# A fused attention and two feed-forward layers on one core: one-bank PSUM tiles for the tanh layer's products, and side work at its two ends moved

## The chip, the core and the metric

The kernel runs on one core of one Trainium2 chip. The metric is device microseconds of one execution, the median of several runs. A core has TensorE (PE in the profile, with its weight loads shown apart as PEld), VectorE (DVE), ScalarE (ACT), GpSimd (POOL) and SyncE (SP, which here issues nearly all DMAs). TensorE writes its products into PSUM, which has eight banks of 512 float32 values per partition; everything else lies in SBUF.

## What is computed

Three layers follow each other, over 4 sequences of 3072 tokens with 256 channels, all in float32:

```python
scores = (1/S) * z @ z.T                  # z: (4, 3072, 64)
x1 = u * (np.maximum(scores, 0)**2 @ v)   # attention, one 3072 x 3072 block per sequence
h  = x1 @ w_in                            # (12288, 256) @ (256, 2048)
x2 = (h - np.tanh(h)) @ w_out             # (12288, 2048) @ (2048, 256): the tanh layer
xk = mu_k*x2 + (1-mu_k)*x2_prev           # x2_prev: the token before, zero at a sequence's start
xr = mu_r*x2 + (1-mu_r)*x2_prev
out = sigmoid(xr @ w_r) * (np.maximum(xk @ w_k, 0)**2 @ w_v)
```

## The kernel before

Every matrix product is taken in three passes of 128x128 by 128x512 over operands split into a high and a low part (`PASSES`), so a product of one 128x128 block is three matmuls. Tokens are worked in 24 tiles of 512. A hand-written order (`tc.manual_schedule()`) sets what stands on each engine's queue; a tile framework adds the waits. An engine works its queue strictly in order, so an instruction that waits holds up all behind it. There are three stages.

Stage A, attention, 288 units (`A`). A unit makes the scores of 256 keys against 512 queries, and its products with `v` are issued two units later (`LAG`). Half of the score blocks are not computed again but loaded back from DRAM transposed; their names are `t` (`h_t`, `l_t`) instead of `A`. Computed blocks that are needed again are transposed by VectorE (`k`) and stored.

Stage S, the tanh layer, 96 units (`h_unit`, called H in the profile's names). A unit n = 8 i + j takes token tiles 2i and 2i+1 and the hidden blocks j and j+8, and computes the four 128x512 blocks of h by seven block products instead of eight. Two PSUM accumulators `e` and `a`, one bank each, hold partial sums, and each of the seven products of three matmuls stands at a fixed place in the unit: `a` gets A11, `e` gets A12; then `a` gets S2 and `e` gets S1; then `e` gets S4 and `a` gets S3; last `a` gets -A22. Between these groups values are taken out: ScalarE copies the first `a` into `r1`, VectorE adds `e` to it; ScalarE copies both into `rc`, and VectorE adds the later `e` and `a` to it crosswise. Tanh is taken of r1 and rc and of the last `a`; VectorE subtracts (`less`), ScalarE takes the high part and VectorE the low part (`h_split`), twice in a unit: `Hx` (h_Hx, l_Hx, of `gx`) and `Hy` (of `gy`). `e` and `a` are the halves of one two-bank tile `w_H`, of which there are two.

The products with `w_out` are issued one unit later, as a list `q` of 24 single matmuls (`h_piece`, six for each of the four blocks of h) that fills TensorE while the other engines empty the accumulators. `cuts` says how many of them stand behind A12, behind S1, and behind S3. In most units the first twelve are Hx pieces; in the unit with j = 0 the list is six Hx pieces, then twelve Hy pieces; with j = 1 the same order. The Hy parts of unit n are made early in unit n+1.

Stage K, the channel mix, per token tile four units `K` and one `R`, again with LAG 2 and squares split into parts.

Side work (loading and splitting weights, preparing x1 as `x`, `xh`, `xd`, `xo`; mixing x2 as `mx`, `mk`, `mr`) is put in by `task(first, last, steps, ...)`: `run_steps(n)` issues steps while a budget per unit lasts, or as many as stand over once `last` has come. `load(n, ...)` issues DMAs at the start of unit n. In the tanh layer `run_steps` is called behind the second group of pieces, so its VectorE steps stand ahead of the `rc` additions. `L718` is the addition into r1, `L738` that into rc, `L631` the copies, `L635` tanh, `L638` the subtraction, `L87` and `L90` the high and low parts, `L625` the block products, `L658` the w_out pieces, `L610` the products of stages A and K, `L562` those of R.

Of the kernel before, what the change touches and what calls it, by code (L numbers as in the profile page):

```python
# [7 lines left out]
F32 = mybir.dt.float32  # L8
# [4 lines left out]
ALU = mybir.AluOpType  # L13

P = 128
# [4 lines left out]
def relu2_attention__tanh_ffn__channel_mix_kernel(  # L20
# [23 lines left out]
    nc = tc.nc  # L44
# [18 lines left out]
    ps = ctx.enter_context(tc.tile_pool(name="ps", bufs=2, space=bass.MemoryType.PSUM))  # L63
# [347 lines left out]
    PASSES = ((0, 0), (0, 1), (1, 0))  # L411
    acc, split = {}, {}

    def work(name):
        return ps.tile([P, 2, 512], F32, tag="wk", name=name, bufs=2)

    def parts(name):
        h = sb.tile([P, 2, 512], F32R, tag="hi", name=f"h_{name}", bufs=3)
# [3 lines left out]
    def scratch(name):  # L422
        return sb.tile([P, 2, 512], F32, tag="e", name=name, bufs=5)
# [164 lines left out]
    def pieces_of(unit):  # L588
        kind, t, p = unit
        if kind == "R":  # L590
            return []
        s = split.pop(unit)
        o = get_acc(kind, t)
        last = {"A": NP, "K": NK}[kind] - 1
        w = []
        for j in range(2):
            f = 2 * p + j
            if kind == "A":
                kp = pairs[t % NG][p]
                f = kp // 2 * 4 + kp % 2 + 2 * j  # L600
                w.append([vs[t // NG, f // 4][:, l, f % 4] for l in range(2)])
            else:
                w.append([x[:, f % 4] for x in ws["v", f // 4]])
        order = [(j, c) for j in range(2) for c in range(DC)]
        if unit == ("K", NT - 1, NK - 1):
            order.sort(key=lambda x: x[1])

        def one(j, c, n):
            a, m = PASSES[n]
            nc.tensor.matmul(  # L610
                o[c],
                w[j][a][:, c * P : (c + 1) * P],
                s[m][:, j],
                start=p == 0 and j == 0 and n == 0,
                stop=p == last and j == 1 and n == 2,
            )

        return [lambda x=(j, c, n): one(*x) for j, c in order for n in range(3)]
# [11 lines left out]
    def copied(t, a):  # L630
        nc.scalar.activation(out=t, in_=a, func=ACTF.Copy)  # L631
        return t
# [4 lines left out]
    def less(g, h):  # L637
        nc.vector.tensor_tensor(out=g, in0=h, in1=g, op=ALU.subtract)  # L638

    def swapped(x):  # L640
        step, n = x.ap[1]
        return bass.AP(x.tensor, x.offset + step, [x.ap[0], (-step, n), *x.ap[2:]])

    hp, hb = {}, {}

    def h_piece(n, half, t):
# [58 lines left out]
    def h_unit(n, q):  # L705

        i, j = divmod(n, NHF)
        if "g" not in hb:
            g = sb.tile([P, 2, 2, 512], F32, tag="big", name="g_H", bufs=12)
            hb["g"] = [g[:, 0], g[:, 1]]  # L710
        gx, gy = hb["g"]
        cuts = [len(q) * 6 // 24, len(q) * 14 // 24]
        w = work(f"w_H{n}")
        e, a = w[:, 0], w[:, 1]
        product(a, i, j, "A11", "B11", True, False)
        product(e, i, j, "A12", "B21", True, True)
        r1 = copied(p2(f"r1_{n}"), a)
        nc.vector.tensor_tensor(out=r1, in0=e, in1=r1, op=ALU.add)  # L718
        if n:
            low = h_split("y")  # L720
            less(gx[:, 0], hb.pop("a"))
            low()
        tanh(gx[:, 1], r1)
        less(gx[:, 1], r1)
        for f in q[: cuts[0]]:
            f()
        product(a, i, j, "S2", "T2", False, False)
        product(e, i, j, "S1", "T1", True, False)
        rc = copied(scratch(f"rc_{n}"), w)
        for f in q[cuts[0] : cuts[1]]:  # L730
            f()
        run_steps(NA + n)
        hb["x"] = (n, 0 if n else 1, 2, ((n - 1, 1, 0) if n else None, (n, 0, 0)), gx)
        low = h_split("x")
        empty()
        product(e, i, j, "S4", "B22", False, True)
        product(a, i, j, "S3", "T3", False, False)
        nc.vector.tensor_tensor(out=swapped(rc), in0=w, in1=swapped(rc), op=ALU.add)  # L738
        low()
        for f in q[cuts[1] :]:  # L740
            f()
        empty()
        tanh(gy, rc)
        less(gy, rc)
        hb["y"] = (n, 0, 2, ((n, 1, 1), (n, 0, 1)), gy)
        product(a, i, j, "-A22", "T4", False, True)
        tanh(gx[:, 0], a)
        hb["a"] = a

    def h_end(n):  # L750
        gx = hb["g"][0]
        low = h_split("y")
        less(gx[:, 0], hb.pop("a"))
        low()
        hb["x"] = (n, 0, 1, ((n - 1, 1, 0), None), gx)
        h_split("x")()
# [83 lines left out]
    NHF = NH  # L840
    NS = NT // 2 * NHF
    units = [("A", t, p) for t in range(NT) for p in range(NP)]
    NA = len(units)
# [3 lines left out]
    NB = NA + NS  # L847
    at = {x: n for n, x in enumerate(units)}
# [19 lines left out]
    for t in range(NT):  # L868
        n = t * NP + (-7 if t % NG == NG - 1 else 1 if t else 5)
# [6 lines left out]
    for b in range(1, B):  # L876
        prev = (b - 1) * NG * NP
        last = prev + (NG - 1) * NP
        for g in range(NG):
            n = last + LAG + (-18, -6, 3, 6, 9, 11)[g]  # L880
            load(n, v_load, b, g)
            task(n + 3, min(n + 12, b * NG * NP + 2 * g + LAG - 2), v_steps, b, g)
        for g in range(NG):
            n = prev + 2 * NP + 7 * g
# [11 lines left out]
    for n, x in enumerate(halves):  # L896
        k = c0 + n * (c1 - c0) // len(halves)
# [4 lines left out]
    def weights(n, end, *x):  # L902
        load(n - (1 if NA < n < NB else 2), w_load, *x, n)
        task(n, end, w_steps, *x)
# [6 lines left out]
    for s in range(2):  # L911
        n = last - 42 + 6 * s
# [6 lines left out]
    for k, n in enumerate((NA + 1, NA + 2, NA + 3, NA + 2)):  # L919
        pieces(n, n, 1, k)  # L920
    weights(NA + 4, NA + 4, "out", 1)
    weights(NA + 4, NA + 4, "out", 3)
    n = NB - NHF
    weights(n + 2, n + 3, "r", 0)
    weights(n + 4, n + 5, "k", 0)
    weights(n + 4, n + 5, "k", 1)
    weights(n + 5, n + 6, "v", 0)
    weights(n + 5, n + 6, "v", 1)
    for i in range(NT // 2):
        n = NA + NHF * i  # L930
        load(n - 6 if i else n - 9, x_load, i)
        task(n - 5 if i else n - 8, n - 1, x_steps, i)
    for i in range(NT):
        n = at["K", i, 0]
        load(n - 5 if i else n - 3, x2_load, i)
        task(n - 4 if i else n - 2, n - 1, mix_steps, "k", i)
        task(n - 3 if i else n - 2, at["R", i, 0] - 1, mix_steps, "r", i)
        n = at["K", i, NK - 1] + LAG
        task(n, n + 2, out_steps, i)
    tasks.sort(key=lambda x: x[:3])  # L940
# [24 lines left out]
    with tc.manual_schedule():  # L965
        z_load(0, 0)
        z_load(0, 1)
        v_load(0, 0)
        z_load(0, 2)
        v_load(0, 1)  # L970

        zeros = scratch("zeros").bitcast(F32R)[:, 0]
        nc.gpsimd.memset(zeros.bitcast(F32), 0.0)
        idle = work("idle")
        for j in range(11):
            nc.tensor.matmul(idle[:, j % 2], zeros[:, :P], zeros, start=True, stop=True)
        for cost, f in z_steps(0, 0) + z_steps(0, 1):
            f()
        for m, src in ((0, moe2_mu_k), (1, moe2_mu_r)):
            with nc.allow_non_contiguous_dma(reason="a column of the mixing vector"):  # L980
                nc.sync.dma_start(out=mu[:, m, :], in_=src.rearrange("(c p) -> p c", p=P))
        def begin(n):
            for f in loads.pop(n, ()):
                f()
            if n in stores:
                stores.pop(n)()

        for n in range(NA):
# [36 lines left out]


# [27 lines left out]
```

## Time and profile before

| | |
|---|---|
| three runs | 2577.86 us median (2577.7 to 2578.09) |
| the profiled execution | 2580.78 us, span 2578.8 us |
| stage A, 0 to 944.9 us | PE busy 938.17, DVE 769.87, ACT 668.81 us; DMA share 0.81 |
| tanh layer, 944.9 to 1971.5 us | PE busy 1013.94, DVE 725.14, ACT 618.60 us; DMA share 0.09 |
| stage K, 1971.5 us to the end | PE busy 597.56, DVE 398.60, ACT 303.32 us; DMA share 0.19 |
| mean granted TensorE clock | 0.997 |
| chain that ended last | PE 90%, DVE 4%, ACT 3%, DMA 1%, issue 1% |

A matmul's busy time is not what it costs. One of 128x512 is shown with about 0.39 us, but the next one starts 0.23 us after it, so they overlap. What TensorE loses shows as a longer step from one start to the next, and only partly as idle time.

### The profile page before, as it was taken

The numbers are of one execution on the slowest core, as the hardware profiler recorded it, in microseconds if no ns is written. First come the engines' busy times: TensorE is split into PE (matmuls) and PEld (weight loads), VectorE is DVE, ScalarE is ACT, GpSimd is POOL, SyncE is SP. The second block draws the span as 40 slices with busy tenths as digits, with TensorE's granted clock in tenths as the row PEclk, the third lists the DMA queues.
The fourth block names the chain that finished last, engine by engine and source line by source line (L and its number), as shares of the span: only waits on it lengthen the run. The fifth ranks groups of instructions, "written<-read, shape, count | busy, mean of one in ns | idle before, by whom it ended". The sixth has DMA issues, their size and how long they took to land.

```text
span 2578.8 us, 29584 instructions
## 1 busy us (share of the span) xinstructions
PE 2549.7 (99%) x11051; PEld 2069.3 (80%) x11051; DVE 1893.6 (73%) x2363; ACT 1590.7 (62%) x1973; POOL 17.5 (1%) x53
## 2 busy tenths in 40 slices
PE   9999999999999999999999999999999999999999
PEld 7888888888888877777777777777777888888887
DVE  8887888888888767677766776677667576676665
ACT  7766776776687666566556655565566455454553
POOL 0000000000000000000000000000000000000000
PEclk9999999999999999999999999999999999999999
DMA  7798689669958860000000000000010112111111
GB/s 192 228 221 216 192 227 226 197 191 238 245 171 277 217 169 28 33 33 15 19 33 34 28 6 33 33 33 1 33 62 25 41 42 49 42 41 45 46 41 33
DMA packets 382784, 260.17 MB, mean 101 GB/s; under 512 B 263984, under 2 KB 337712, under 8 KB 382640
## 3 DMA queue, kind: packets, MB, share of 16 engines
q1 hardware_dynamic: 379472, 257.89, 36.9%
q8 instruction: 86, 1.41, 0.2%
q10 hardware_dynamic: 3168, 0.39, 0.1%
q14 instruction: 58, 0.48, 0.1%
HBM read 142.87 MB, written 109.31 MB: 98 GB/s over the span
## 4 chain that ended last, share of the span: by engine, by line
PE 90%; DVE 4%; ACT 3%; DMA 1%; issue 1%; SPq 0%; ACTq 0%; DVEq 0%
PE acc_A L610 29%; PE w_H L625 19%; PE acc_H L658 15%; PE w_K L547 10%; PE acc_K L610 10%; PE w_A L524 3%; PE w_A L523 3%; PE w_R L562 3%; DVE r L718 3%; ACT r L631 2%; DMA b<-at 1%; DMA zin<-in_z_dram 0%; SPq L105 0%; DVE rc L738 0%; DVE xo_T L90 0%
## 5 line engine op out<-in xcount | busy, mean ns | idle before, releaser
L610 PE MATMUL acc_A<-h_A,v 128*128 128x512 f32 x1344 | 441.1, 390 | 0.3 <-ACT h_A L87 0.3
L625 PE MATMUL w_H<-xo_T,w_in 128*128 128x512 f32 x1152 | 322.1, 401 | 12.7 <-DVE rc L738 5.3
L610 PE MATMUL acc_A<-h_t,v 128*128 128x512 f32 x960 | 309.8, 389 | 0.0
L610 PEld LDWEIGHTS acc_A<-h_A,v 128*128 128x128 f32 x1344 | 253.1, 188 | 53.3 <-ACT h_A L87 0.8
L430 ACT ACTIVATE a_A<-w_A 128x1024 f32<-128x1024 f32 (+1 forms) x169 | 172.8, 1022 | 197.8 <-PE w_A L524 197.1
L625 PEld LDWEIGHTS w_H<-xo_T,w_in 128*128 128x128 f32 x1152 | 208.5, 188 | 95.0 <-DVE r L718 47.9
L658 PE MATMUL acc_H<-h_Hx,w_out 128*128 128x512 f32 x768 | 268.1, 390 | 0.0
L610 PE MATMUL acc_A<-l_A,v 128*128 128x512 f32 x672 | 262.4, 390 | 2.5 <-DVE l_A L90 2.5
L658 PE MATMUL acc_H<-h_Hy,w_out 128*128 128x512 f32 x768 | 252.7, 390 | 0.0
L610 PE MATMUL acc_K<-h_K,w_v 128*128 128x512 f32 x768 | 252.1, 389 | 0.0
L547 PE MATMUL w_K<-mkh,w_k 128*128 128x512 f32 x768 | 248.3, 389 | 0.0
L90 DVE TENSOR_TENSOR l_A<-a_A,h_A 128x1024 fp32r<-128x1024 f32 (+1 forms) x169 | 201.8, 1194 | 61.0 <-ACT h_A L87 60.2
L430 ACT ACTIVATE a_K<-w_K 128x1024 f32<-128x1024 f32 x96 | 98.2, 1023 | 223.0 <-PE w_K L547 223.0
L738 DVE TENSOR_TENSOR rc<-w_H,rc 128x1024 f32<-128x1024 f32 x96 | 117.4, 1223 | 135.4 <-PE w_H L625 135.4
L458 DVE STREAM_TRANSPOSE k<-a_A 128x512 f32<-128x512 f32 x240 | 156.0, 689 | 77.4 <-ACT a_A L431 75.8
L610 PEld LDWEIGHTS acc_A<-h_t,v 128*128 128x128 f32 x960 | 180.2, 188 | 37.4
L635 ACT ACTIVATE g_H<-rc 128x1024 f32<-128x1024 f32 x96 | 101.9, 1062 | 168.7 <-DVE rc L738 168.7
L434 DVE CAST h_K<-a_K 128x1024 fp32r<-128x1024 f32 x96 | 66.5, 692 | 187.1 <-ACT a_K L431 181.8
L610 PE MATMUL acc_A<-l_t,v 128*128 128x512 f32 x480 | 186.7, 389 | 0.0
L431 ACT ACTIVATE a_A<-a_A 128x1024 f32<-128x1024 f32 (+1 forms) x169 | 178.4, 1056 | 5.4
L87 ACT ACTIVATE h_t<-b 128x512 fp32r<-128x512 f32 x240 | 136.7, 619 | 65.0 <-PE acc_A L610 48.3
L658 PEld LDWEIGHTS acc_H<-h_Hx,w_out 128*128 128x128 f32 x768 | 144.2, 188 | 30.7
(154 smaller groups left out, 4981.5 us busy)
## 6 DMA issues: line engine op xcount, KB each, us to landing
at<-k SPq DMA_DIRECT2D x120, 512.0 KB, 3.6
b<-at SPq DMA_DIRECT2D x240, 256.0 KB, 6.5
vr<-in_v_dram SPq DMA_DIRECT2D x24, 512.0 KB, 7.4
uin<-in_u_dram SPq DMA_DIRECT2D x192, 64.0 KB, 2.8
x1d<-x SPq DMA_DIRECT2D x24, 512.0 KB, 3.3
x<-x1d SPq DMA_DIRECT2D x24, 512.0 KB, 5.1
x2d<-x SPq DMA_DIRECT2D x48, 256.0 KB, 2.1
x<-x2d SPq DMA_DIRECT2D x24, 512.0 KB, 3.2
```

The lines of the kernel that those rows point to most:

```text
L87: nc.scalar.activation(out=o, in_=i, func=ACTF.Copy)
L90: nc.vector.tensor_tensor(out=o, in0=i, in1=hi.bitcast(F32), op=ALU.subtract)
L430: nc.scalar.activation(out=a[:, x], in_=w[:, x], func=ACTF.Relu, scale=sc)
L431: nc.scalar.activation(out=a[:, x], in_=a[:, x], func=ACTF.Square)
L458: nc.vector.transpose(out=t[:, :, :, c].rearrange("p b a j -> p a b j"), in_=a[:, c].rearrange("p (a b i) -> p a b i", a=4, b=4),)
L523: nc.tensor.matmul(w[:, j], lhsT, z1[b, g], start=True, stop=False)
L547: nc.tensor.matmul(w[:, j], ws["k", f // 4][a][:, c, (f % 4) * P : (f % 4 + 1) * P], x[m][:, c], start=n == 0, stop=n == 3 * DC - 1,)
L610: nc.tensor.matmul(o[c], w[j][a][:, c * P : (c + 1) * P], s[m][:, j], start=p == 0 and j == 0 and n == 0, stop=p == last and j == 1 and n ...
L625: nc.tensor.matmul(o, w[l][:, (j % 4) * P : (j % 4 + 1) * P], x[m], start=first and k == 0, stop=last and k == 2, skip_group_check=True,)
L635: nc.scalar.activation(out=g, in_=h, func=ACTF.Tanh)
L658: nc.tensor.matmul(o[c], ws["out", f // 4][a][:, f % 4, c * P : (c + 1) * P], hp[n, half, t][m], start=bool(first and k == 0), stop=bool(l ...
L738: nc.vector.tensor_tensor(out=swapped(rc), in0=w, in1=swapped(rc), op=ALU.add)
```

## The change

It has three parts. First, the accumulators of the tanh layer become tiles of their own, `we` and `wa`, one bank and two buffers each. The pool of the two-bank work tiles is closed at the end of stage A, a pool for the tanh layer takes its banks, and a third pool takes them for stage K (`rooms`). The copy into rc becomes two copies, the addition two additions, and since rc is no longer filled crosswise the two names of `hb["y"]` change places. Second, the cuts: 8 pieces behind A12 where there were 6 (6 still with j = 1), 7 behind S1 where there were 8, 9 behind S3 where there were 10. Third, side work: x1 of the first pair of tiles is loaded and prepared nine units earlier, in stage A; one `w_out` part goes a unit later; the weights of stage K go three or more units later each, `v` into stage K itself; and the mixing of the first tile of stage K is spread over the last eight units of the tanh layer.

```diff
+    banks = {}
+    def rooms(name):
+        if "pool" in banks:
+            banks.pop("pool").__exit__(None, None, None)
+        if name:
+            banks["pool"] = tc.tile_pool(name=name, bufs=2, space=bass.MemoryType.PSUM)
+            banks["ps"] = banks["pool"].__enter__()
+
     def work(name):
-        return ps.tile([P, 2, 512], F32, tag="wk", name=name, bufs=2)
+        return banks["ps"].tile([P, 2, 512], F32, tag="wk", name=name, bufs=2)
+
+    def bank(which, n):
+        return banks["ps"].tile([P, 512], F32, tag=which, name=f"{which}_{n}", bufs=2)
...
-        cuts = [len(q) * 6 // 24, len(q) * 14 // 24]
-        w = work(f"w_H{n}")
-        e, a = w[:, 0], w[:, 1]
+        cuts = [6 if j == 1 else len(q) * 8 // 24, len(q) * 15 // 24]
+        e, a = bank("we", n), bank("wa", n)
...
-        rc = copied(scratch(f"rc_{n}"), w)
+        rc = scratch(f"rc_{n}")
+        copied(rc[:, 0], a)
+        copied(rc[:, 1], e)
...
-        nc.vector.tensor_tensor(out=swapped(rc), in0=w, in1=swapped(rc), op=ALU.add)
+        for k, x in enumerate((e, a)):
+            nc.vector.tensor_tensor(out=rc[:, k], in0=x, in1=rc[:, k], op=ALU.add)
...
-        hb["y"] = (n, 0, 2, ((n, 1, 1), (n, 0, 1)), gy)
+        hb["y"] = (n, 0, 2, ((n, 0, 1), (n, 1, 1)), gy)
...
-    weights(NA + 4, NA + 4, "out", 3)
+    weights(NA + 5, NA + 5, "out", 3)
+    for n, x in ((-3, ("r", 0)), (-3, ("k", 0)), (-2, ("k", 1)), (-1, ("v", 0)), (0, ("v", 1))):
+        weights(NB + n, NB + n + 1, *x)
     for i in range(NT // 2):
         n = NA + NHF * i
-        load(n - 6 if i else n - 9, x_load, i)
-        task(n - 5 if i else n - 8, n - 1, x_steps, i)
+        load(n - 6 if i else n - 18, x_load, i)
+        task(n - 5 if i else n - 17, n - 1 if i else n - 6, x_steps, i)
     for i in range(NT):
         n = at["K", i, 0]
-        load(n - 5 if i else n - 3, x2_load, i)
+        load(n - 5 if i else n - 9, x2_load, i)
...
```

TensorE's queue in the tanh layer, unit 40 (j = 0), from the second half of the A12 product on; h_Hy and l_Hy are the parts made in this same unit. Before:

```order
L625 MATMUL w_H_11262<-xh_11086,w_in_0_7415 128x512
L658 MATMUL acc_H_10824<-h_Hx_11235,w_out_8708 128x512
L658 MATMUL acc_H_10824<-l_Hx_11236,w_out_8708 128x512
L658 MATMUL acc_H_10824<-h_Hx_11235,w_out_8708 128x512 x2
L625 MATMUL w_H_11262<-xo_T_11089,w_in_1_7786 128x512 x3
L625 MATMUL w_H_11262<-xo_T_11158,w_in_1_7786 128x512 x3
L658 MATMUL acc_H_10792<-h_Hy_11272,w_out_8706 128x512
L658 MATMUL acc_H_10792<-l_Hy_11273,w_out_8706 128x512
```

The same place of the change:

```order
L637 MATMUL we_11389<-xh_11207,w_in_0_7418 128x512
L666 MATMUL acc_H_10933<-h_Hx_11362,w_out_8804 128x512
L666 MATMUL acc_H_10933<-l_Hx_11363,w_out_8804 128x512
L666 MATMUL acc_H_10933<-h_Hx_11362,w_out_8804 128x512 x2
L666 MATMUL acc_H_10900<-h_Hy_11400,w_out_8730 128x512
L666 MATMUL acc_H_10900<-l_Hy_11401,w_out_8730 128x512
L637 MATMUL wa_11390<-xo_T_11210,w_in_1_7789 128x512 x3
L637 MATMUL we_11389<-xo_T_11282,w_in_1_7789 128x512 x3
```

In this unit the two pieces added ahead of S2 and S1 are Hy pieces, the second of which reads l_Hy; before, the first six matmuls of S2 and S1 stood ahead of them.

VectorE's queue in stage A, the units of token tile 22 that compute key pairs 7 and 10; `k` are the transposes of a computed block, `l_A` its low part, which TensorE reads; `xd` and `x` belong to the preparation of x1 of tiles 0 and 1. Before:

```order
L173 STREAM_TRANSPOSE uT_7958<-uin_7806 128x1024
L458 STREAM_TRANSPOSE k_4_10_7978<-a_A_7_7973 128x4x4x32 x2
L90 TENSOR_TENSOR l_A_7_7975<-a_A_7_7973,h_A_7_7974 128x1024
L90 TENSOR_TENSOR l_t_8_7996<-b_4_2_7815,h_t_8_7995 128x512 x2
L90 TENSOR_TENSOR l_t_9_8015<-b_4_3_7884,h_t_9_8014 128x512 x2
L173 STREAM_TRANSPOSE uT_8047<-uin_7917 128x1024
L458 STREAM_TRANSPOSE k_4_11_8049<-a_A_10_8042 128x4x4x32 x2
L90 TENSOR_TENSOR l_A_10_8044<-a_A_10_8042,h_A_10_8043 128x1024
```

The same place of the change:

```order
L173 STREAM_TRANSPOSE uT_7965<-uin_7809 128x1024
L369 TENSOR_TENSOR xd_T_7985<-x_7948,x_7947 128x512
L369 TENSOR_TENSOR xd_T_7987<-x_7948 128x512
L470 STREAM_TRANSPOSE k_4_10_7989<-a_A_7_7980 128x4x4x32 x2
L90 TENSOR_TENSOR l_A_7_7982<-a_A_7_7980,h_A_7_7981 128x1024
L90 TENSOR_TENSOR l_t_8_8007<-b_4_2_7818,h_t_8_8006 128x512 x2
L369 TENSOR_TENSOR xd_T_8029<-x_7948,xd_T_7985 128x512
L90 TENSOR_TENSOR l_t_9_8026<-b_4_3_7887,h_t_9_8025 128x512 x2
L369 TENSOR_TENSOR xd_T_8045<-xd_T_8029,x_7947 128x512
L90 TENSOR_TENSOR x_7947<-x_7947,xh_8062 128x1024
L470 STREAM_TRANSPOSE k_4_11_8065<-a_A_10_8057 128x4x4x32 x2
L90 TENSOR_TENSOR l_A_10_8059<-a_A_10_8057,h_A_10_8058 128x1024
```

Two steps that read the x just loaded now stand ahead of the transposes of block 7, and the subtraction of `xh`, a copy that ScalarE makes behind the square of block 10, stands ahead of those of block 10.

TensorE's queue at the end of the tanh layer with its waits; the last `-A22` product, and the first product of stage K. Before:

```order
L658 MATMUL acc_H_14819<-l_Hy_15231,w_out_8708 128x512
L658 MATMUL acc_H_14819<-h_Hy_15230,w_out_8708 128x512
L625 MATMUL w_H_15220<-xo_T_14682,w_in 128x512 [waits DVE_49]
L625 MATMUL w_H_15220<-xo_T_14682,w_in 128x512 x2
L547 MATMUL w_K_0_15308<-mkh_15266,w_k_15047 128x512 [waits PE_49]
```

The same place of the change:

```order
L666 MATMUL acc_H_15099<-l_Hy_15537,w_out_8804 128x512
L666 MATMUL acc_H_15099<-h_Hy_15536,w_out_8804 128x512
L637 MATMUL wa_15526<-xo_T_14955,w_in 128x512 [waits DVE_49]
L637 MATMUL wa_15526<-xo_T_14955,w_in 128x512 x2
L559 MATMUL w_K_0_15614<-mkh_15116,w_k_15421 128x512 [waits DVE_49]
```

The first product of stage K now has a wait on VectorE. The instruction that it waits for is the subtraction of the last `wa` (`less(gx[:, 0], ...)` in `h_end`), since its tile lies on banks of the pool just closed.

## Rows read from the trace of the kernel before

**Rows 1.** The waits: who waited for whom, us, times, longest.

```profile
PEld w_H L625 <- DVE r L718: 47.9, 96, 0.9
PEld w_H L625 <- DVE rc L738: 7.7, 6, 3.6
```

**Rows 2.** Timeline of PE, unit 43: start us, us, what.

```profile
1406.92 0.39 PE L625 MATMUL w_H<-xh,w_in 128*128 128x512 f32 x1
...
1411.35 0.40 PE L658 MATMUL acc_H<-h_Hx,w_out 128*128 128x512 f32 x1
...
1417.49 0.39 PE L625 MATMUL w_H<-xh,w_in 128*128 128x512 f32 x1
```

**Rows 3.** Timeline of ACT, unit 43.

```profile
1408.48 0.60 ACT L631 ACTIVATE r<-w_H 128x512 f32<-128x512 f32 x1 [0.76 <-PE w_H L625]
...
1411.61 1.03 ACT L631 ACTIVATE rc<-w_H 128x1024 f32<-128x1024 f32 x1 [1.06 <-PE w_H L625]
```

**Rows 4.** Timeline of PE and DVE, unit 40 (j = 0).

```profile
1374.90 0.39 PE L625 MATMUL w_H<-xh,w_in 128*128 128x512 f32 x1
...
1377.14 0.69 DVE L718 TENSOR_TENSOR r<-w_H,r 128x512 f32<-128x512 f32 x1 [1.35 <-ACT r L631]
...
1379.63 0.49 PE L658 MATMUL acc_H<-l_Hy,w_out 128*128 128x512 f32 x1
1379.96 0.39 PE L658 MATMUL acc_H<-h_Hy,w_out 128*128 128x512 f32 x1
```

**Rows 5.** Timeline of DVE and PE, unit 7.

```profile
1023.85 0.68 DVE L369 TENSOR_TENSOR xd_T<-x,x 128x512 f32<-128x512 f32 x1
...
1030.73 1.21 DVE L738 TENSOR_TENSOR rc<-w_H,rc 128x1024 f32<-128x1024 f32 x1
...
1032.00 1.65 PE L625 MATMUL w_H<-xo_T,w_in 128*128 128x512 f32 x3 [3.23 <-DVE rc L738]
...
1035.72 0.40 PE L658 MATMUL acc_H<-h_Hx,w_out 128*128 128x512 f32 x1
```

**Rows 6.** Windows: window, us, busy of the five engines, PEclk, DMA share, GB/s.

```profile
1032.00:1036.00 4.00, 4.00 (x11) 3.19 (x12) 2.30 (x2) 1.73 (x3) 0.00 (x0) 0.58 0.00 0
```

**Rows 7.** Timeline of PE, stage K's first R unit.

```profile
1994.37 0.39 PE L610 MATMUL acc_K<-h_K,w_v 128*128 128x512 f32 x1
1996.93 0.47 PE L562 MATMUL w_R<-mrh,w_r 128*128 128x512 f32 x1 [2.17 <-DVE mrh L799]
...
2005.32 0.40 PE L610 MATMUL acc_K<-l_K,w_v 128*128 128x512 f32 x1
```

**Rows 8.** Timeline of SP, DVE and PE, the end of stage A.

```profile
893.30 0.47 SPq L132 DMA_DIRECT2D z<-z  x1
...
896.40 1.30 DVE L458 STREAM_TRANSPOSE k<-a_A 128x512 f32<-128x512 f32 x2 [2.66 <-ACT a_A L431]
...
899.72 0.39 PE L610 MATMUL acc_A<-l_A,v 128*128 128x512 f32 x1
...
906.70 1.18 DVE L90 TENSOR_TENSOR l_A<-a_A,h_A 128x1024 fp32r<-128x1024 f32 x1
...
908.78 0.39 PE L610 MATMUL acc_A<-l_A,v 128*128 128x512 f32 x1
...
915.83 1.20 SPq L360 DMA_DIRECT2D x<-x1d  x2
...
923.51 0.69 DVE L369 TENSOR_TENSOR xd_T<-x,x 128x512 f32<-128x512 f32 x1 [1.01 <-DMA x<-x1d]
...
939.49 0.50 PE L610 MATMUL acc_A<-l_A,v 128*128 128x512 f32 x1 [1.53 <-DVE l_A L90]
```

**Rows 9.** Timeline of ACT and DVE, the last unit and the end of the layer.

```profile
1964.08 1.03 ACT L631 ACTIVATE rc<-w_H 128x1024 f32<-128x1024 f32 x1 [1.07 <-PE w_H L625]
...
1969.39 1.22 DVE L738 TENSOR_TENSOR rc<-w_H,rc 128x1024 f32<-128x1024 f32 x1
...
1972.94 0.68 DVE L638 TENSOR_TENSOR g_H<-w_H,g_H 128x512 f32<-128x512 f32 x1
```

**Rows 10.** DMA issues by line: count, KB each, median us to landing.

```profile
x<-x1d SPq DMA_DIRECT2D x24, 512.0 KB, 5.1
```

More of the change, by code (lines that the diff above doesn't have):

```diff
@@ L638, in less @@
         nc.vector.tensor_tensor(out=g, in0=h, in1=g, op=ALU.subtract)
-    def swapped(x):
-        step, n = x.ap[1]
-        return bass.AP(x.tensor, x.offset + step, [x.ap[0], (-step, n), *x.ap[2:]])
     hp, hb = {}, {}
@@ L921, in relu2_attention__tanh_ffn__channel_mix_kernel @@
     weights(NA + 4, NA + 4, "out", 1)
-    weights(NA + 4, NA + 4, "out", 3)
[L923 to L928, printed above, removed]
+    weights(NA + 5, NA + 5, "out", 3)
+    for n, x in ((-3, ("r", 0)), (-3, ("k", 0)), (-2, ("k", 1)), (-1, ("v", 0)), (0, ("v", 1))):
+        weights(NB + n, NB + n + 1, *x)
     for i in range(NT // 2):
         n = NA + NHF * i
-        load(n - 6 if i else n - 9, x_load, i)
-        task(n - 5 if i else n - 8, n - 1, x_steps, i)
+        load(n - 6 if i else n - 18, x_load, i)
+        task(n - 5 if i else n - 17, n - 1 if i else n - 6, x_steps, i)
     for i in range(NT):
         n = at["K", i, 0]
-        load(n - 5 if i else n - 3, x2_load, i)
-        task(n - 4 if i else n - 2, n - 1, mix_steps, "k", i)
-        task(n - 3 if i else n - 2, at["R", i, 0] - 1, mix_steps, "r", i)
+        load(n - 5 if i else n - 9, x2_load, i)
+        task(n - 4 if i else n - 8, n - 1 if i else n - 7, mix_steps, "k", i)
+        task(n - 3 if i else n - 7, at["R", i, 0] - 1 if i else n - 4, mix_steps, "r", i)
         n = at["K", i, NK - 1] + LAG
@@ L973, in relu2_attention__tanh_ffn__channel_mix_kernel @@
         nc.gpsimd.memset(zeros.bitcast(F32), 0.0)
+        rooms("ps_a")
         idle = work("idle")
@@ L1000, in relu2_attention__tanh_ffn__channel_mix_kernel @@
                 run_steps(n)
+        rooms("ps_h")
         q = [f for u in units[NA - LAG : NA] for f in pieces_of(u)]
@@ L1012, in relu2_attention__tanh_ffn__channel_mix_kernel @@
         h_end(NS)
+        rooms("ps_k")
         for n in range(NB, len(units) + LAG + 3):
@@ L1023, in relu2_attention__tanh_ffn__channel_mix_kernel @@
             run_steps(n)
+        rooms(None)
         assert not loads and not tasks and not ready
```

## The prediction

> **What bounds the kernel now.** The chain that ended last is TensorE for 90% of the span, so I look for what TensorE loses. The waits come first: its weight loads wait 96 times, once in every unit of the tanh layer, for the addition into r1, and six times for the addition into rc [rows 1]. How much a wait costs is read in the timeline, from start to start. In unit 43 the matmul at 1411.35 and the next unit's first at 1417.49 are 27 matmuls apart, 6.14 us, so a step is 0.2274 us; from 1406.92 to 1411.35 there are 18, which should take 4.09 and take 4.43 [rows 2]. The unit loses 0.34 us, all of it at the gate behind A12. What makes the gate is ScalarE's copy: it starts 1.56 us into the unit [rows 3], when the second half of the tile is written too, although the half that it reads was ready three matmuls earlier. The addition follows 2.24 us into the unit [rows 4], and S2 and S1 wait for it. Below I count time from a unit's start and call a step 0.2274; an undisturbed unit of 45 matmuls is 10.23 us.
>
> The other losses are single. [...] The first R unit of stage K waits twice for mr; from 1994.37 to 2005.32, 16 matmuls, 10.95 us go where 3.64 would do, a loss of 7.3 [rows 7]. At the end of stage A TensorE idles 1.53 us for a low part [rows 8].
>
> **What the change takes away.** *The gate.* With a tile of its own the copy of `a` needs A11 alone and can start at about 0.9, and r1's addition needs only A12 and that copy: 1.6 instead of 2.24, done by 2.3. The order puts 8 pieces (6 with j = 1) behind A12, so S2 stands at 14 steps, 3.18 (j = 1: 2.73), and S1 three steps later. Nothing waits there: 96 x 0.34 = 32.6 us. *The rc waits.* The six cost 7.7 us less a step each, since a weight load waits from a step earlier: 6.3, and 1.67 of slow clock: 8.0 us. *l_Hy.* In units with j = 0 and 1 the step behind the first l_Hy piece is 0.33 instead of 0.23 [rows 4]; 23 of them give 2.3. *R.* mr of the first tile is now made in units 88 to 92, so all 7.3 go. *End of stage A.* The x steps that stood before that low part are gone: 1.5. Together 51.7 us.
>
> **What the split itself costs.** Two copies of 512 take 2 x 0.60 where one of 1024 took 1.03 [rows 3], two additions 2 x 0.69 [rows 4] for 1.21 [rows 5]: 0.17 us on each of two engines. Both have cover. S1 ends at about 4.7, the copy of `e` at 5.35; S4 stands at 27 steps, 6.14. S3's last result is there at 7.7, the addition of `wa` ends at 8.4 at the earliest, and -A22 stands at 42 steps, 9.55, so 1.15 us of lateness is free. [...] If both halves lay on TensorE's path, 96 x 0.34 us would take back the gate's whole gain; that is the last rival below.
>
> **What it adds.** *Hy pieces too early.* In the units with j = 0 the two pieces moved ahead of S2 are h_Hy and l_Hy of this very unit. From the start of r1's addition to the l_Hy matmul it takes 1379.63 - 1377.14 = 2.49 us [rows 4] (the addition, one subtraction, l_Hy itself). With the addition at 1.6 that is 4.1; TensorE comes to this piece at 13 steps, 2.96. Everything behind it, S2 first, stands 1.14 us, in 11 units (unit 0 has other pieces): 12.5 us. Bounds 0.9 to 1.4 each.
>
> *Unit 7.* Two of the ten side steps have gone to units 3 and 4. Against before, the steps start 0.63 earlier and are 1.2 shorter, but now stand about 0.55 for `xh`, which ScalarE makes only after both copies (5.35 + 1.05); the additions are 0.1 longer to their end, and -A22 stands 0.34 earlier. 3.39 (the idle time and what a step is longer) - 0.63 - 1.2 + 0.55 + 0.1 + 0.34 = 2.5. Whether the clock falls behind it no row tells: between nothing and the 1.67 behind 3.23 us of idle time I take 0.7, and 3.2 together.
>
> *Unit 89* gets the four steps mxk, mxr, mkh, mkl, as the last unit had four. There the copy into rc ended at 1965.11 and the addition began at 1969.39 [rows 9], 4.28 later. From 5.35 that gives 9.63, and 1.3 for two additions 10.95: 1.4 us late. Unit 95, freed of them, has a single weight part and is in time.
>
> *Into stage K.* The first K product now waits for the last `less` of the layer. From the start of the rc addition to its end it took 1973.62 - 1969.39 = 4.23 us [rows 9]; from `wa`'s addition alone, 0.5 less. With the weight part ahead of it (copy to 6.4, low part to 7.6, first addition to 8.25) it ends at 11.95; the product would start at 10.23. 1.7 us.
>
> *Stage A.* The loads of x now stand on SP behind `uin`, where `z` was issued at 893.30 [rows 8]: x at 893.3 and 893.8. Landing takes 5.1 us by the median of 24 [rows 10], or, from issue to the first step in this stage, 923.51 - 915.83 = 7.7. The second lands at 898.9 to 901. The two steps that read it are ahead of block 7's transposes on VectorE, which before began at 896.40. Two steps of 0.60, transposes 1.23, l_A 1.18: TensorE's l_A matmul, before at 899.72, can go at 902.5 to 904.6, 2.8 to 4.9 us late (2.3 if x lands by 898.4). I take 2.8, as nothing else is queued behind `uin`, and 0.9 of slow clock: 3.7. Three units later the `xh` copy (1.05) and its subtraction (1.14) stand before block 10's transposes: l_A, done at 907.88 before, is 2.2 later, and its matmul at 908.78 loses 1.3.
>
> **The sum.** Added: 12.5 + 3.2 + 1.4 + 1.7 + 3.7 + 1.3 = 23.8. 51.7 - 23.8 = 27.9 us less. The profiled execution took 2580.78, so 2552.9; the runs' median lies 2.9 below it, so 2550.0. Uncounted are some tenths: unit 0, which loses less than before, and units with five side steps.
>
> **Rivals.** *The new waits are covered.* If x lands in 5.1 or less and the clock holds, and the K product waits for its own bank alone, 3.7 + 1.3 + 1.7 + 3 of the additions go: 2540. The TensorE order speaks against more: the l_Hy wait is in it. Without that too, 2526 would be the floor.
>
> *The additions run on.* Each x step of stage A delays what follows it on VectorE, whose low parts TensorE reads with about 1 us to spare [rows 8]. If x lands like the slowest here and each of three later blocks is late as well, with a slow clock each time, it is 4.9 + 3 x 1.3 + 4 x 1.67 = 15 instead of 5, and with 1.4 in each j = 0 unit and 0.05 us left over per unit at the two gates, 2550 + 10 + 3 + 5 = 2568.
>
> *It does not do what it says.* If the copy of `a` still waited for `e`, S2 at 3.18 would nevertheless find r1 done at 2.94; only the 12 units with j = 1 (S2 at 2.73) would lose, 2.5 us, and j = 0 units 0.6 each more: 2559.
>
> *Slower: the rc additions decide.* Their place is in front of -A22, and they have 1.15 us to spare. If copies and additions came that much later in every unit (ScalarE's order rc(a), rc(e), side work, h_Hx behind a late tanh of r1), the split's 0.34 would be paid 96 times, 32.6 us: 2582.6. For it speaks that -A22 stands nearer than before; against it that before, with the same engines as full, this addition is named as releaser only six times in 96 units [rows 1].
>
> **How the numbers follow.** My forecast, with its own range 2542 to 2561: 0.72, with the case that the copy still waits (0.04 of it). Covered waits: 0.10. Additions that run on: 0.13. Additions that decide, or a wait that I did not see in the 96 units: 0.05. For 8 in 10 I go to 2540 and 2564. About 0.2%, 5 us, is what a measurement of this kernel can tell from no change; faster thus means below 2572.7. That takes the first two cases and nearly all of the third: 0.94. Same 0.03, slower 0.03.
>
> **What would show it.** The 96 waits for r1's addition gone from the list of waits; units with j other than 0 at 10.2 us, those with j = 0 at 11.4, standing for l_Hy behind the seventh piece; waits for the `wa` addition in units 7 and 89 alone; the first K product waiting for a subtraction; no wait in the first R unit; and at 899 to 905 a wait for l_A, behind xd steps that end on the landing of x. It is wrong if VectorE's adds end most waits throughout the layer, or if j = 0 units are no longer than the others.

## The result, and the profile after

The changed kernel takes 2553.4 us (median of 4 runs, 2552.67 to 2554.4) where the kernel before, measured beside it, takes 2577.98 (2577.7 to 2579.12): a ratio of 0.9904, 95% interval 0.9887 to 0.9921, or 24.6 us less. The forecast was 2550.0 in a range of 2540 to 2564. The profiled execution took 2552.99 us with a span of 2551.1.

Where the 27.7 us between the two profiled spans come from, with each stage's length taken from its first matmul to the next stage's:

| kernel (profiled run) | stage A | tanh layer | stage K | unit 7 | unit 8 | a later j = 0 | j = 1 | j = 2 to 4 |
|---|---|---|---|---|---|---|---|---|
| before | 943.6 | 1026.6 | 607.3 | 14.72 | 11.62 | 10.75 | 10.71 | 10.57 |
| changed | 950.3 | 999.2 | 600.4 | 12.60 | 12.55 | 11.49 | 10.25 | 10.20 |

The tanh layer gains 27.4 and stage K 7.0, and stage A gives 6.7 back. In the list of waits of the weight loads (who waited for whom, us, times, longest us) the 96 for the addition into r1 [rows 1] are gone, four for that into rc are left (in units 0, 7, 15 and 89), and others have come:

```profile
PEld acc_H L666 <- DVE l_Hy L90: 14.4, 11, 1.4
PEld acc_A L622 <- DVE l_A L90: 9.7, 3, 7.1
PEld wa L637 <- DVE rc L748: 4.1, 4, 2.5
...
PEld w_K L559 <- DVE g_H L650: 1.9, 1, 1.9
```

The timeline of the changed kernel (start us, us, engine, line, what, and in brackets the idle time with its releaser), first unit 40 with j = 0, then unit 43:

```profile
1367.58 0.39 PE L637 MATMUL wa<-xh,w_in 128*128 128x512 f32 x1
...
1369.19 0.69 DVE L725 TENSOR_TENSOR r<-we,r 128x512 f32<-128x512 f32 x1 [1.02 <-PE we L637]
...
1370.30 0.40 PE L666 MATMUL acc_H<-h_Hy,w_out 128*128 128x512 f32 x1
1371.67 0.50 PE L666 MATMUL acc_H<-l_Hy,w_out 128*128 128x512 f32 x1 [0.97 <-DVE l_Hy L90]
...
1399.52 0.39 PE L637 MATMUL wa<-xh,w_in 128*128 128x512 f32 x1
...
1400.20 0.39 PE L637 MATMUL we<-xh,w_in 128*128 128x512 f32 x1
1400.40 0.60 ACT L643 ACTIVATE r<-wa 128x512 f32<-128x512 f32 x1
1400.42 0.39 PE L637 MATMUL we<-x,w_in 128*128 128x512 f32 x1
1400.65 0.39 PE L637 MATMUL we<-xh,w_in 128*128 128x512 f32 x1
...
1402.69 0.84 PE L637 MATMUL wa<-xo_T,w_in 128*128 128x512 f32 x3
...
1409.72 0.39 PE L637 MATMUL wa<-xh,w_in 128*128 128x512 f32 x1
```

In unit 43 the copy of `a` starts 0.88 us into the unit, where it took 1.56 [rows 2, 3], and S2 follows 14 steps in, without a wait; the unit takes 10.20 us. In unit 40 r1's addition starts at 1.61, and the l_Hy piece at 4.09 instead of the 2.95 at which its turn comes.

Stage A, and below it the three largest single waits of the tanh layer (unit 7, unit 89, the step into stage K):

```profile
892.24 0.97 SPq L360 DMA_DIRECT2D x<-x1d  x2
...
901.53 0.69 DVE L369 TENSOR_TENSOR xd_T<-x,x 128x512 f32<-128x512 f32 x1 [9.19 <-DMA x<-x1d]
...
902.74 1.30 DVE L470 STREAM_TRANSPOSE k<-a_A 128x512 f32<-128x512 f32 x2
903.96 1.19 DVE L90 TENSOR_TENSOR l_A<-a_A,h_A 128x1024 fp32r<-128x1024 f32 x1
...
905.20 0.80 PE L622 MATMUL acc_A<-l_A,v 128*128 128x512 f32 x1 [6.72 <-DVE l_A L90]
...
913.57 1.22 DVE L90 TENSOR_TENSOR x<-x,xh 128x1024 fp32r<-128x1024 f32 x1 [4.81 <-ACT xh L87]
...
917.16 0.50 PE L622 MATMUL acc_A<-l_A,v 128*128 128x512 f32 x1 [1.06 <-DVE l_A L90]
```

```profile
1033.74 0.96 PE L637 MATMUL wa<-xo_T,w_in 128*128 128x512 f32 x3 [2.12 <-DVE rc L748]
...
1887.13 0.96 PE L637 MATMUL wa<-xo_T,w_in 128*128 128x512 f32 x3 [0.27 <-DVE rc L748]
...
1950.74 0.50 PE L559 MATMUL w_K<-mkh,w_k 128*128 128x512 f32 x1 [1.44 <-DVE g_H L650]
```

Every place of the second fence is one that the prediction named; the waits for rc in units 0 and 15, 0.44 and 0.37 us on the weight loads, it did not name. In the first, VectorE stands 9.19 us in front of an xd step, because the second half of x has landed only 9.3 us after the pair's issue; the transposes behind the two steps, the low part and TensorE's matmul follow in a row, and TensorE loses 6.9 us.

### The profile page after: what moved, and what is told of

Same layout as the page of the kernel before. It is cut to its first block, busy times and chain, and to the rows that moved or that the text cites. A ratio compares the mean times of both kernels' runs of the same rounds, so it can differ in the third digit from the quotient of the medians.

```text
span 2551.1 us, 29895 instructions
## 1 busy us (share of the span) xinstructions
PE 2519.0 (99%) x11051; PEld 2076.0 (81%) x11051; DVE 1903.4 (75%) x2459; ACT 1611.0 (63%) x2069; POOL 16.6 (1%) x53
## 4 chain that ended last, share of the span: by engine, by line
PE 96%; DVE 2%; ACT 1%; SPq 0%; issue 0%; DMA 0%; DVEq 0%; POOL 0%; ACTq 0%; POOLq 0%
PE acc_A L622 30%; PE acc_H L666 19%; PE w_K L559 10%; PE acc_K L622 10%; PE wa L637 10%; PE we L637 8%; PE w_A L536 3%; PE w_A L535 3%; PE w_R L574 3%; DVE l_Hy L90 0%; DVE g_H L650 0%; DMA x<-x1d 0%; DVE r L725 0%; SPq L164 0%; PE idle L983 0%
## 5 line engine op out<-in xcount | busy, mean ns | idle before, releaser
L666 PE MATMUL acc_H<-h_Hy,w_out 128*128 128x512 f32 x768 | 268.0, 390 | 0.0
L666 PE MATMUL acc_H<-h_Hx,w_out 128*128 128x512 f32 x768 | 256.4, 390 | 0.1
L637 PE MATMUL wa<-xo_T,w_in 128*128 128x512 f32 x864 | 243.3, 390 | 2.4 <-DVE rc L748 2.4
L637 PEld LDWEIGHTS wa<-xo_T,w_in 128*128 128x128 f32 x864 | 161.4, 188 | 37.7 <-DVE rc L748 4.1
L559 PEld LDWEIGHTS w_K<-mkh,w_k 128*128 128x128 f32 x768 | 144.1, 188 | 31.8 <-DVE g_H L650 1.9
```

The costliest lines, as they stand in the source:

```text
L559: nc.tensor.matmul(w[:, j], ws["k", f // 4][a][:, c, (f % 4) * P : (f % 4 + 1) * P], x[m][:, c], start=n == 0, stop=n == 3 * DC - 1,)
L637: nc.tensor.matmul(o, w[l][:, (j % 4) * P : (j % 4 + 1) * P], x[m], start=first and k == 0, stop=last and k == 2, skip_group_check=True,)
L666: nc.tensor.matmul(o[c], ws["out", f // 4][a][:, f % 4, c * P : (c + 1) * P], hp[n, half, t][m], start=bool(first and k == 0), stop=bool(l ...
```

## The experiments

Times are medians; the kernel before took 2578.2 us beside experiments 1 to 4, 2578.63 beside 5 to 8 and 2578.88 beside 9 to 11. Stage and unit lengths are of the profiled runs.

| | run | us | stage A | tanh layer | stage K | unit 7 | unit 8 | a later j = 0 |
|---|---|---|---|---|---|---|---|---|
| 1 | tiles only | 2541.24 | 941.7 | 988.7 | 609.3 | 14.22 | 12.31 | 10.21 |
| 2 | cuts only | 2572.56 | 941.8 | 1019.5 | 606.1 | 14.07 | 12.09 | 12.10 |
| 3 | side work only | 2575.64 | 949.8 | 1022.8 | 600.2 | 12.87 | 11.85 | 10.75 |
| 4 | changed, 6 pieces for j = 0 | 2539.15 | 949.1 | 985.7 | 600.4 | 12.60 | 11.83 | 10.21 |
| 5 | 4 + x loaded earlier | 2530.12 | 941.5 | 984.2 | 600.3 | 12.60 | 10.26 | 10.21 |
| 6 | 4 + x where it was before | 2532.94 | 941.9 | 987.4 | 600.3 | 13.58 | 11.83 | 10.21 |
| 7 | 4 + side work spread | 2536.63 | 950.9 | 982.4 | 600.3 | 10.20 | 10.23 | 10.20 |
| 8 | 4 + 5 + 7 | 2527.36 | 941.3 | 982.5 | 600.3 | 10.20 | 10.25 | 10.20 |
| 9 | cuts only, 6 pieces for j = 0 | 2558.07 | 941.8 | 1006.2 | 606.8 | 14.72 | 11.65 | 10.75 |
| 10 | 8, spread more finely | 2526.39 | 941.2 | 981.4 | 600.3 | 10.21 | 10.23 | 10.21 |
| 11 | 10 with the cuts of before | 2525.23 | 941.3 | 980.4 | 600.3 | 10.21 | 10.25 | 10.23 |

### 1 to 3: each part alone

Each is the kernel before with one part of the change: the one-bank tiles with their pools, copies and additions; the line of the cuts; or the lines of the side work (by which the weights of stage K go one to three units later, not three or more each).

> The kernel before with the one-bank tiles alone; cuts of 6 and 14 pieces and the side work stay as before. My theory: the tile by itself opens the gate behind A12. S2 stands at 12 steps, 2.73 us, and r1 is added by 2.3, so no unit waits there (in the changed kernel the units with j = 1, which also have 6 pieces, take 10.25 us); the first l_Hy piece stands behind S1 and waits for nothing. All 96 units lose the 0.37 us and some, units at 10.2 with j = 0 no longer than the others; the losses at the end of stage A, in unit 7 and at the first R stay. 2538 to 2543 us. Rival: the longer cut is what covers r1's addition, and with 6 pieces S2 waits about 0.2 us in every unit: 2555 to 2562.

> The kernel before with the new cuts alone (8, 6 with j = 1, and 15); the two-bank tile and the side work stay. My theory: r1 is added 2.93 us into the unit as before, but S2 now stands at 14 steps, 3.18, so the gate opens by the cuts too, except in the 12 units with j = 1, which keep 0.34. The l_Hy piece ahead of S2 comes at 2.96 and is ready only at about 4.7, so 11 units with j = 0 lose 1.8 or 1.9 each, 20 us: 2578 - 30 - 2 + 20 = 2566, 2562 to 2570. Rival: the tile is what opens the gate, and with two banks in one tile the units keep 10.57: then only the l_Hy wait is added, about 2595.

> The kernel before with the moved side work alone. My theory: stage A is 6 to 7 us longer (950 instead of 944 us, the wait for l_A at 898 us and the low clock behind it), the waits for mr in the first R unit (7.3) go, unit 7 loses 2 to 3 us less, the last unit's rc wait of 1.4 goes and unit 89 gets about 1: 2572 to 2576, nearly nothing for all of it. Rival: the wait in stage A belongs to the changed kernel's other timing, and x lands in about 5 us here: 2566 to 2569.

The ratios to before are 0.9858 (0.9843 to 0.9872), 0.9978 (0.9969 to 0.9988) and 0.9989 (0.998 to 0.9999). The tiles alone are 12 us faster than all three parts together, although they bring a cost of their own at the step into stage K: TensorE idles 2.05 us in front of the first K product, with a granted clock of 0.70 from 1931 to 1936 us; unit 95 takes 13.51 us instead of 12.12, and stage K is 2.0 longer. The waits of the weight loads with the tiles only:

```profile
PEld wa L637 <- DVE rc L748: 5.7, 5, 3.5
PEld w_R L574 <- issue: 2.6, 1, 2.6
PEld w_K L559 <- DVE g_H L650: 2.5, 1, 2.5
PEld acc_A L622 <- DVE l_A L90: 2.5, 2, 1.9
```

and with the cuts only:

```profile
PEld acc_H L658 <- DVE l_Hy L90: 17.9, 23, 1.3
PEld w_H L625 <- DVE rc L738: 15.3, 16, 4.0
PEld acc_H L658 <- ACT h_Hy L87: 8.2, 11, 0.7
PEld w_H L625 <- DVE r L718: 6.2, 13, 0.5
```

With the tiles no wait for r1 or l_Hy is left although only six pieces stand behind A12. With the cuts alone the wait for r1 falls from 96 to 13, in unit 0 and the units with j = 1, which keep six pieces, so the gate opens there too, by having TensorE arrive later; but the Hy pieces now come before h_Hy as well, and the rc additions end 16 waits instead of 6. This part came out slower than my 2562 to 2570: I had counted no new rc waits, nine of which stand in units with j = 5, most of which stay at 10.58 us. The side work pays in stage K and in units 7 and 95 a little more than it costs in stage A and unit 89; 2575.64 is within what was expected.

### 4 and 9: which cut, with and without the tiles

```diff
-        cuts = [6 if j == 1 else len(q) * 8 // 24, len(q) * 15 // 24]
+        cuts = [6 if j < 2 else len(q) * 8 // 24, len(q) * 15 // 24]
```

Experiment 4 makes this edit in the changed kernel, experiment 9 puts the new line into the kernel before.

> The changed kernel with 6 pieces behind A12 in the units with j = 0 too (as with j = 1), so that no Hy piece stands ahead of S2. My theory: the l_Hy wait, 11 times 1.29 us by the unit lengths, goes whole, since S2 finds r1 ready at 2.73 us and the l_Hy piece then comes at 4.5 us when l_Hy is ready at about 4.2: 2539, 2538 to 2541. Rival 1: the wait moves to l_Hy's new place and half remains: 2546. Rival 2: S2 waits for r1 in these units, no gain or less than 3 us: 2550 to 2554.

> The kernel before, two-bank tile and old side work, with the new cuts in the units with j of 2 to 7 and 6 pieces behind A12 where j is 0 or 1. My theory: the cut and the tile are two ways to open one gate. Units with j of 2 to 4 and 6 take 10.2 us as with the new cuts alone, those with j = 0 and 1 stay at 10.75 and 10.7, where only a tile of its own would help, and j = 5 keeps its 10.6: 2572.6 less 11 times 1.36, 2557.6, 2556 to 2560; of the 37 us of the tiles the cuts alone then give 20. Rival: S2 two or three steps later pushes the rc additions against -A22 in more units, now that the l_Hy wait no longer makes room in front of them: 2562 or more.

Both came out within 0.5 us of what was expected. In 4 the 11 waits for l_Hy are gone and the units with j = 0 take 10.21 us; 14.2 us of the change's time was this one number. In 9 the weight loads still wait like this:

```profile
PEld w_H L625 <- DVE rc L738: 15.3, 16, 4.0
PEld w_H L625 <- DVE r L718: 11.9, 24, 0.5
```

The 24 waits for r1 are those of the 12 units with j = 0 and the 12 with j = 1. So the tile does what the cut does not: it opens the gate in all units, with six pieces, and leaves the Hy pieces where they were.

### 5 and 6: x of the first pair

```diff
-        load(n - 6 if i else n - 18, x_load, i)
+        load(n - 6 if i else n - 20, x_load, i)
```

for experiment 5; in 6 the loads and steps stand at `n - 9`, `n - 8` and `n - 1`, as before the change.

> The version with 6 pieces for j = 0, and the loads of x of the first pair two units earlier on SP's queue, ahead of the eight uin transfers; the steps that read x stay where they are. My theory: x lands 9 us after its issue because the DMA engines are full there (share 1.09 and 1.06 from 882 to 892 us), so that the issue and not the steps decides; issued at about 884 it is there at 893, before the steps' place, and the wait for l_A at 898 us goes with the low clock behind it, 7.8 us; the 1.2 of the xh subtraction stays. Stage A 941 to 942 us, 2531.4, 2530 to 2533. Rival 1: the two xd steps themselves delay the transposes behind them, 1.3 to 2 us stay: 2533 to 2535. Rival 2: uin or b land later instead and TensorE waits for them: 2536 or more.

> The version with 6 pieces for j = 0, and x of the first pair loaded and prepared where it was before, in the last nine units of stage A. My theory: nothing is gained by the nine units at all; stage A is as long as with the tiles alone (941.7 us, with 1.7 of wait at its end) instead of 949.1, and unit 7 is as before this edit: 2531.7, 2530 to 2534. Rival: unit 0 and the end of stage A lose what is gained, 2536 or more.

The timeline of experiment 5:

```profile
884.52 0.93 SPq L360 DMA_DIRECT2D x<-x1d  x2
885.50 10.57 SPq L164 DMA_DIRECT2D uin<-in_u_dram  x8
...
894.15 0.69 DVE L369 TENSOR_TENSOR xd_T<-x,x 128x512 f32<-128x512 f32 x1 [1.97 <-DMA x<-x1d]
894.75 0.69 DVE L369 TENSOR_TENSOR xd_T<-x 128x512 f32<-128x512 f32 x1
895.36 1.30 DVE L470 STREAM_TRANSPOSE k<-a_A 128x512 f32<-128x512 f32 x2
896.58 1.18 DVE L90 TENSOR_TENSOR l_A<-a_A,h_A 128x1024 fp32r<-128x1024 f32 x1
...
898.15 0.39 PE L622 MATMUL acc_A<-l_A,v 128*128 128x512 f32 x1
```

It is 9.6 us from x's issue to the step here too, but the issue is 7.7 us earlier, and l_A is ready 0.4 us before TensorE reads it. Stage A is 7.6 us shorter than in 4, and no wait came up elsewhere. The rest of the 9.0 us is mostly unit 8, where the granted clock did not fall this time (1.00 from 1025.9 to 1029.9 us; in 4 it was 0.57 from 1033.5 to 1037.5); nothing shows that the edit did that. The loads are slow, I take it, because they meet others; no run tests that by itself. The windows of the changed kernel (window, us, busy of the five engines, granted clock, DMA share, GB/s) around x's issue:

```profile
882.00:888.00 6.00, 6.00 (x28) 4.99 (x27) 1.70 (x3) 4.15 (x5) 0.00 (x0) 1.00 1.09 269
888.00:892.00 4.00, 4.00 (x20) 3.30 (x19) 3.57 (x6) 1.19 (x3) 0.00 (x0) 1.00 1.06 167
```

Experiment 6, 2532.94, shows that stage A is as short with x where it was before. What the later place costs against 5 is 1.0 in unit 7 (13.58 instead of 12.60) and 0.6 in unit 15 (11.04 instead of 10.43); unit 8 (11.83 instead of 10.26) is slow again, as in 4: its matmuls that start from 1027.78 to 1029.92 us are shown with 0.63 us, where 0.39 is usual. So the nine units are worth about 1.6 us, once x lands in time.

### 7, 8 and 10: the side work spread

```diff
-        left = {"A": 2.0, "S": 1.4, "K": 2.4, "R": 4.0}[kind] + spare[0]
+        left = {"A": 2.0, "S": 2.4 if n < NA + NHF else 1.4, "K": 2.4, "R": 4.0}[kind] + spare[0]
...
-        task(n - 4 if i else n - 8, n - 1 if i else n - 7, mix_steps, "k", i)
-        task(n - 3 if i else n - 7, at["R", i, 0] - 1 if i else n - 4, mix_steps, "r", i)
+        task(n - 4 if i else n - 8, n - 1 if i else n - 4, mix_steps, "k", i)
+        task(n - 3 if i else n - 7, at["R", i, 0] - 1 if i else n - 2, mix_steps, "r", i)
```

Experiment 8 adds the earlier load; 10 has 2.2 in place of 2.4, and `n - 5` in place of `n - 7` for the start of "r".

> The version with 6 pieces for j = 0, with the side work of units 0 to 7 taken at a budget of 2.4 per unit instead of 1.4, and the mixing of the first tile of stage K due three units (mk) and two units (mr) later: unit 7 has two steps instead of eight, unit 89 two instead of four, none more than three. My theory: units 7, 8, 15 and 89 take 12.60, 11.83, 10.44 and 11.17 us where 10.2 would do; all of it goes, 5.2 us, the low clock in unit 8 with the wait in unit 7: 2534, 2533 to 2535. Rival: three steps in units 4 to 6 are late too, 0.3 to 0.5 each: 2535 to 2536.5.

> Six pieces for j = 0, x loaded two units earlier, and the side work spread as in the run before. My theory: the three losses have separate places and add up: 2539.15 - 7.8 - 5.2 = 2526.2, 2525 to 2528; left are 1.2 at 915 us, 1.6 at the first K product, and the first 20 us. Rival: one of them covers the other or comes back elsewhere, 2529 or more.

> One-bank tiles, 6 pieces for j = 0 and 1, x loaded two units earlier, the first units' budget 2.2 instead of 2.4 and mr from unit 91 on: in unit 5 an xd step of 0.69 stands ahead of w_out's low part in place of the x subtraction of 1.22, which had to wait for ScalarE's xh, and unit 89 has one mxk and mkh instead of mxk and mxr. My theory: the 1.47 us of unit 5 and the 0.4 of unit 89 go, 2527.4 - 1.9 = 2525.5, 2524.5 to 2526.5. Rival: the x subtraction is as late in unit 6 or 7 and takes there what unit 5 gives back: 2527.

Units 7, 8 and 15 came down to 10.2 as expected, but experiment 7 gained 2.5 instead of 5.2 us: its rival, side steps that are late in units 4 to 6, came true. Unit 5 takes 11.68, unit 89 still 10.62 (the weight load of a w_out piece waits there 0.5 us for a copy on ScalarE), and stage A happened to be 1.7 longer than in 4. Experiment 8 came out within its 2525 to 2528. In unit 5 (timeline of experiment 8) another side step is what is late:

```profile
999.99 1.23 DVE L90 TENSOR_TENSOR x<-x,xh 128x1024 fp32r<-128x1024 f32 x1 [2.61 <-ACT xh L87]
1001.13 1.22 DVE L90 TENSOR_TENSOR w_out<-wr_out,w_out 128x1024 fp32r<-128x1024 f32 x1
...
1002.40 0.73 PE L666 MATMUL acc_H<-h_Hy,w_out 128*128 128x512 f32 x2 [0.90 <-DVE w_out L90]
```

VectorE waits 2.61 us for ScalarE's xh, and w_out, which the pieces of this unit read, stands behind it. With the x subtraction moved to unit 6 (experiment 10) unit 5 takes 10.20 and unit 6 10.80: 1.0 us gained of the 1.9 expected, the rest of it lost as the rival said.

### 11: the tiles with the cuts of before

```diff
-        cuts = [6 if j < 2 else len(q) * 8 // 24, len(q) * 15 // 24]
+        cuts = [len(q) * 6 // 24, len(q) * 14 // 24]
```

> The same with the cuts of before, 6 and 14 in every unit. My theory: with the tiles the cuts decide nothing, r1 is added before 2.73 us: the same time as the run with 6 pieces for j = 0 and 1 alone, within 1 us. Rival: the room that 8 pieces give covers something in the ordinary units, and they are 0.03 us or more longer: 2528 or more.

2525.23 us, ratio to before 0.9793 (0.9779 to 0.9806), 1.2 us faster than 10, where no more than 1 was expected: with the tiles the new cuts decide nothing in the ordinary units, which stay at 10.20, and cost half a microsecond in unit 6, which takes 10.34 here. This is the fastest version. Of the weight loads' waits inside the tanh layer one is left:

```profile
PEld w_K L559 <- DVE g_H L650: 1.8, 1, 1.8
...
PEld wa L637 <- DVE rc L748: 0.3, 1, 0.3
```

## Why the prediction was right, step by step

**The gate** was right in its place, times and cause: the copy at 0.88 (0.9), r1's addition at 1.61 (1.6), S2 without a wait at 14 steps. Its size was 0.37 us per unit, 10.57 to 10.20, instead of 0.34: I had taken the step of 0.2274 from the undisturbed half of a unit, and the undisturbed unit's is 10.20 / 45 = 0.2267. Over 96 units that is 2.9 us. What the prediction did not separate is which part opens the gate. It put both, earlier copy and longer cut, into one sum, although its own times for j = 1 (six pieces, S2 at 2.73, r1 done by 2.3) said that the tile would do; experiments 1, 2 and 11 show that the tile alone does it, and that the cut beside it costs.

**The split's cost** was covered, as said. Two copies took 599 and 598 ns on average and two additions 689 and 688 ns, which is 0.17 and 0.16 us more than the single ones, and ordinary units have no wait for rc, so in the layer's time they do not show. As for the gate's opening, the copy of `wa` at 1400.40 takes its 0.60 us while TensorE writes `we`, by the matmuls shown at 1400.20, 1400.42 and 1400.65; so what held the copy in the kernel before was the common tile, and not that TensorE was writing.

**l_Hy** was right as a mechanism and nearly in size: l_Hy's piece at 4.09 (4.1), 1.14 late (1.14), and 0.11 us more in the step behind it, so that a unit takes 1.29 more. 11 of them are 14.2, instead of 12.5. The 0.11 is the longer step behind an l_Hy piece that the prediction had booked as gone in these units too.

**The other places of the layer.** Unit 7: 2.40 and 1.06 of low clock in unit 8 (2.5 and 0.7; the granted clock is 0.57 from 1034.6 to 1038.6 us); the l_Hy wait of unit 8 hides part of it, and in experiment 4, without that wait, unit 8 loses 1.6. Unit 89: 0.92 (1.4), part of it behind a copy on ScalarE (0.48 on the weight load) that the prediction did not have. Into stage K: a step of 1.83, 1.6 lost (1.7). R: no wait is left there [rows 7], and stage K is 6.96 us shorter (7.3). The 1.67 of slow clock, counted among the rc waits as saved, is measured in unit 7 of before: behind 3.23 us of idle time nine matmuls, 1032.00 to 1035.72, take 3.72 us where nine steps are 2.05 [rows 2, 5], at a granted clock of 0.58 from 1032 to 1036 [rows 6]. In the changed kernel the clock fell again, behind 2.12 us.

**Stage A** is the term that was wrong in size, and its failing step is the landing of x. I wrote that the second half lands at 898.9 to 901 and took 2.8 us of lateness, the end that goes by the median of 24 loads; it landed at 901.4, the step that reads it began at 901.53, and the wait cost 6.9, with 1.6 of low clock behind it (0.9 forecast, an estimate that no row gave): eight steps take 3.45 instead of 1.81 us, at a granted clock of 0.52. The upper end of 4.9 did not hold it either, for TensorE also came to that matmul 1.4 us earlier than in the trace of before, at 898.3 instead of 899.72 [rows 8]. The xh subtraction cost 1.2 (1.3). What should have warned me stands in the trace of before, in the window where eight uin transfers are issued: a DMA share of 1.02, where the tanh layer, which has 22 of the 24 loads in that median, has 0.09.

```profile
880.00:890.00 10.00, 10.00 (x46) 8.29 (x45) 5.70 (x8) 5.71 (x8) 0.00 (x0) 1.00 1.02 255
```

What the slow landings have in common is the stage. The second half of the first pair landed 7.2 us after its own issue in the kernel before, 8.7 in the changed one (behind uin), 9.0 in experiment 5 (ahead of uin) and 9.9 in experiment 6 (at 914 us, with no uin near it). That the full DMA engines are the reason is argued, not shown; the share alone does not tell it, for the z load of 128 KB that stood at x's place before [rows 8] landed after 2.2 us, where each half of x has 512 KB.

**The sum.** For the profiled execution 2552.9 was forecast and 2552.99 measured, which is partly luck: stage A was 3.2 us longer than its terms say and the tanh layer 3.3 shorter. The runs' median is 3.4 us above the forecast, because I carried over that before's profiled execution lay 2.9 us above its median. That was no property of the kernel: its stage A took 943.6 us, where 941.7 to 941.9 were measured in four runs with the same side work in that stage. That is 1.8 of the 2.9; the rest is open. Of the rivals none held. Of "The additions run on" the slow landing came, beyond the 4.9 that it allowed, but only the one later block that the forecast had counted was late. "It does not do what it says" came nearest to asking the right question, since S2 14 steps in finds r1 done even with the late copy.

## What to carry to other kernels

When two edits open the same gate, run each alone: here the one that made TensorE arrive later brought its own wait into every eighth unit and hid that the other was enough. Before a piece of work is moved ahead on an engine's queue, look up when its operand is made in the same unit, and for a load also how long such a load takes to land in that stage: the second half of the first x took 7.2 to 9.9 us in stage A, where the median of all 24 is 5.1. A step that must wait for another engine should not stand ahead of one that TensorE is about to read: in unit 5 of experiment 8 VectorE waited 2.61 us for such a step, and TensorE 0.90 behind it.

## What the runs showed of the hardware

The same wait had two prices. In the changed kernel TensorE idles 2.12 us in front of -A22 of unit 7, and the granted clock is 0.57 from 1034.6 to 1038.6 us, with 0.50 from 1034.8 to 1038.0; in experiment 5 it idles 2.12 us at the same product and the clock is 1.00 from 1025.9 to 1029.9. The window of the changed kernel, then the matmul and the window of experiment 5:

```profile
1034.60:1038.60 4.00, 4.00 (x12) 3.14 (x11) 2.84 (x5) 3.02 (x5) 0.00 (x0) 0.57 0.00 0
```

```profile
1025.08 0.96 PE L637 MATMUL wa<-xo_T,w_in 128*128 128x512 f32 x3 [2.12 <-DVE rc L748]
```

```profile
1025.90:1029.90 4.00, 4.00 (x19) 3.33 (x18) 3.86 (x6) 3.34 (x6) 0.00 (x0) 1.00 0.00 0
```

Twelve matmuls pass in the first 4 us and nineteen in the second. Experiments 2 and 9 are such a pair too, with longer idle times in front of the same product at the same place, and there the three matmuls themselves show it:

```profile
1029.25 0.96 PE L625 MATMUL w_H<-xo_T,w_in 128*128 128x512 f32 x3 [3.60 <-DVE rc L738]
```

```profile
1029.24 1.65 PE L625 MATMUL w_H<-xo_T,w_in 128*128 128x512 f32 x3 [3.59 <-DVE rc L738]
```

In 2 they take 0.96 us, in 9 they take 1.65. So the length of this idle time alone does not decide. It may differ between executions of one kernel as well: two of experiment 5 took 2529.42 and 2529.66 us with a mean granted clock of 1.000, the other two 2530.59 and 2530.65 with 0.998; where in the kernel these lost it, no trace shows. No run here tells what decides; a forecast has to carry both. The 1.6 us into stage K were not tried away: the first product of the new pool waits for the last reader of the old one, 1.44 us at 1950.74.
